# The last gate's weights in two transfers, and ScalarE's group loop as a hardware loop

## The chip, the cores and the metric

The kernel runs on one core of a Trainium2 chip. The metric is the device time of one execution in microseconds. The time before is the median of three runs. The profile is of one more execution, whose own time is given beside its span.

Names used below: PE is TensorE, PEld its weight loads, DVE is VectorE, ACT is ScalarE, POOL is GpSimd, SP is SyncE, which here issues nearly all DMAs. Sixteen DMA engines carry the transfers. Code that an engine has not yet loaded arrives over the same DMA engines, in the profile's queues of kind "instruction".

## What is computed

One decode step of a transformer block for four sequences (B = 4, D = 512), all in f32. A conditioning vector c gives six modulation vectors through one matrix:

```python
mod = (_silu(c) @ w_mod).reshape(c.shape[0], 6, 1, -1)
sa, ca, ga, sb, cb, gb = (mod[:, 0], mod[:, 1], mod[:, 2], mod[:, 3], mod[:, 4], mod[:, 5])
h = _layernorm(x, axis=-1) * (1 + ca) + sa
x = x + ga * _A_ref(h, A_k_cache, A_v_cache, A_wq, A_wo)
h = _layernorm(x, axis=-1) * (1 + cb) + sb
x = x + gb * _B_ref(h, B_w1, B_w3, B_w2)
```

A is attention of one new token over the last 2048 positions of a cache, with 32 query heads of 128 in 8 groups of 4 that share a key and a value head. B is a gated MLP (silu(h w1) * (h w3)) w2 with 1792 hidden columns. The change touches the last gate, gb: columns 2560 to 3071 of w_mod, a product of silu(c) (4 x 512) with a 512 x 512 block.

## The kernel before

**Data and stages.** About 101 MB are read once: for each of the 8 groups 4 MB of keys and 4 MB of values, then the projections, the modulation matrix and the MLP's weights. They arrive in three SBUF buffers: KV[0] and KV[1] (64 KB a partition each), used by even and odd groups, and WP (32 KB) for query and output projections of a pair of groups. In the last stage KV[0] takes the middle modulation weights (wm_in) and w1 with part of w3 (f1_in), KV[1] the rest of w3 (f2_in), the last gate's weights (gb_in, 1 MB) and w2 (w2_in, 3.5 MB in six pieces).

**Who waits for what.** Every engine's program is written out by hand, with semaphores. SP issues the loads in a fixed order (L89 in the helper `load`); before a load that overwrites a buffer it waits until the last reader is done: for WP until the pair's queries are projected (`q_done`) and the pair before has its output projected (`a_done`), for KV until the group's value products are done (`o_done`). PE runs the groups as a hardware loop over four pairs (bodies "pair" and "query"). It takes its inputs with a wait that counts the semaphore down again (`take`, L269), so that one piece of code serves all rounds. DVE and ACT run the eight groups written out one after another (`weights(g)`) and wait on counts that grow from group to group.

**A group.** PE makes the scores (bS), DVE the row maxima and their negative (NB), ACT the exponentials p_sb with their sums (L230), PE turns them (`turn`, L287), DVE places them (pT), PE forms the products with the values (bO, `o_done`), DVE makes the reciprocal sums (LB), ACT scales (o_sb, L251), PE turns the result (bX, `x_done`), DVE picks the diagonal (oT) and PE projects it into bA (`a_done`). For the next group's queries PE projects (bQ, `q_done`), ACT scales (q_sb, L201), PE turns (bT, `qt_done`) and DVE places them into Z (L206).

**The gates.** c comes in t0_in as 16 columns: k-th block of 128 inputs for the 4 sequences. ACT and DVE make silu of it (L182 to L188) in `sc`. For the last gate PE multiplies `sc` block k with block k of the weights into rows 32k to 32k+3 of bank bM, four products of 512 columns side by side (L446). ACT copies bM (L448); a product with the 0/1 matrix `same` later adds the four partial rows up.

**The end.** The six pieces of w2 are consumed in the order of their landing; the partial results of the first eight chunks (bO) are folded (y_sb, `same`) into bX beside the last six. Then DVE multiplies with the gate and adds the residual (L478, L480), SP stores (L482).

Of the kernel before, what the change touches and what calls it, by code (L numbers as in the profile page):

```python
# [5 lines left out]
AF = mybir.ActivationFunctionType  # L6
ALU = mybir.AluOpType
AX = mybir.AxisListType
ET = mybir.EngineType

B, D, HQ, G, SK, DH, W, FF = 4, 512, 32, 8, 8192, 128, 2048, 1792
P = 128
# [2 lines left out]
EPS = 1e-5  # L15
CHUNKS = [(j, c) for c in range(4) for j in range(4) if c < 2 or j < 3]
HEAD = 8
W2_CUTS = [0, 4, 8, 10, 12, 13, 14]
PAIRS = G // 2

# [20 lines left out]
        return (self.sem, self.n)  # L41


def block_kernel(nc, x_in, t0_in, t1_in, kv_in, w_in, wm_in, f1_in, f2_in, gb_in, w2_in, out):
    T, v, s, gp, S = nc.tensor, nc.vector, nc.scalar, nc.gpsimd, nc.sync

    def sems(names):
        return [nc.alloc_semaphore(n) for n in names.split()]

    def sb(name, cols, rows=P):  # L50
        return nc.alloc_sbuf_tensor(name, (rows, cols), F32).ap()
# [5 lines left out]
    A = Queue(nc, s, "act")  # L57
    V = Queue(nc, v, "dve")
    L = Queue(nc, gp, "pool")
    dx, dt0, dt1, dkv, dk, dva, dvb, dwo, dm, df1, df2a, df2b, dgb = sems("dx dt0 dt1 dkv dk dva dvb dwo dm df1 df2a df2b dgb")  # L60
    dw = sems(" ".join(f"dw{i}" for i in range(len(W2_CUTS) - 1)))
    z_ok, q_ok, p_ok, k_ok, va_ok, vb_ok, pt_ok, o_ok, ot_ok = sems("z_ok q_ok p_ok k_ok va_ok vb_ok pt_ok o_ok ot_ok")
    s_done, q_done, qt_done, pp_done, o_done, x_done, a_done, pe, last = sems("s_done q_done qt_done pp_done o_done x_done a_done pe last")
    (dout,) = sems("dout")

    KV = [sb("KV0", 16384), sb("KV1", 16384)]
    WP = sb("WP", 8192)
    T0 = KV[1][:, : 16 + 4096]
    x_sb = sb("x_sb", 512, B)
    ident, same, eps = sb("ident", P), sb("same", B), sb("eps", 1)  # L70
    sc, e1, e2 = sb("sc", 16), sb("e1", 16), sb("e2", 16)
    hT, h2T = sb("hT", 16), sb("h2T", 16)
    Z = sb("Z", B * 28)
    q_sb, p_sb, o_sb, a_sb, y_sb, g_sb, u_sb, gb_sb = [sb(n, 512) for n in "q_sb p_sb o_sb a_sb y_sb g_sb u_sb gb_sb".split()]
# [13 lines left out]
    def load(dst, src, sem):  # L88
        S.dma_start(dst, src).then_inc(sem, 16)  # L89
# [7 lines left out]
    for p in range(PAIRS):  # L97
        if p == PAIRS - 1:
            break
        S.wait_ge(q_done, 2 * p + 2)  # L100
        if p:
            S.wait_ge(a_done, 2 * p)
        if p < PAIRS - 2:
            load(WP, w_in[p], dwo)
        else:
            load(WP, w_in[p], dwo)
        S.wait_ge(o_done, 2 * p + 1)
        load(KV[0], kv_in[2 * p + 2], dkv)
        S.wait_ge(o_done, 2 * p + 2)
        if p < PAIRS - 2:  # L110
            load(KV[1], kv_in[2 * p + 3], dk)
    S.wait_ge(a_done, G - 2)
# [1 line left out]
    load(KV[1][:, :8192], kv_in[G - 1][:, :8192], dk)  # L114
    load(KV[1][:, 8192:14336], kv_in[G - 1][:, 8192:14336], dva)
    load(KV[1][:, 14336:], kv_in[G - 1][:, 14336:], dvb)
    S.wait_ge(o_done, G - 1)
    load(KV[0][:, :6144], wm_in, dm)
    load(KV[0][:, 6144:14336], f1_in, df1)
    S.wait_ge(o_done, G)  # L120
    load(KV[1][:, :3072], f2_in[:, :3072], df2a)
    load(KV[1][:, 3072:6144], f2_in[:, 3072:], df2b)
    load(KV[1][:, 6144:8192], gb_in, dgb)
    for a, b, sem in zip(W2_CUTS[:-1], W2_CUTS[1:], dw):
        load(KV[1][:, 8192 + a * 512 : 8192 + b * 512], w2_in[:, a * 512 : b * 512], sem)


    l_eps = L.op(gp.memset(eps, EPS))
# [50 lines left out]
    v_same = V.op(v.tensor_reduce(same, ident.rearrange("p (j i) -> p i j", i=32)[:, :B, :], axis=AX.X, op=ALU.add))  # L179

    A.wait((dt0, 16))
    t = A.op(s.activation(e1, T0[:, :16], AF.Exp, scale=-1.0))  # L182
    V.wait(t)
    t = V.op(v.tensor_scalar(e2, e1, 1.0, None, op0=ALU.add))
    V.wait(t)
    t = V.op(v.reciprocal(e2, e2))
    V.wait(t, (dt0, 16))
    t_sc = V.op(v.tensor_mul(sc, T0[:, :16], e2))  # L188

    A.wait((pe, 1))  # L190
    t_sa = A.op(s.copy(sa_sb, bM[32 : 32 + B, :]))
# [3 lines left out]
    t_h = V.op(v.scalar_tensor_tensor(h, xs, st1[:, 7:8], sa_sb, op0=ALU.mult, op1=ALU.add))  # L195
    V.wait((pe, 2))
    t_hT = V.op(v.tensor_copy(hT, bT[:, :16]))  # L197

    def q_evac(g):
        A.wait((q_done, g + 1), v_z)  # L200
        A.op(s.mul(q_sb, bQ, DH**-0.5), q_ok)  # L201

    def q_place(g):
        V.wait((qt_done, g + 1), l_z)
# [15 lines left out]
    def weights(g):  # L220
        V.wait((s_done, g + 1), l_z)
        t = V.op(v.reduce_max(MX[:, 0:1], bS, axis=AX.X))  # L222
        V.wait(t)
        t = V.op(v.transpose(MT, MX))
        V.wait(t)
        t = over_t(NM, MT, ALU.max, negate=True)
        V.wait(t)
        t_nm = V.op(v.transpose(NB, NM))  # L228
        A.wait(t_nm)
        A.op(s.activation(p_sb, bS, AF.Exp, bias=NB[:, 0:1], accum_out=SM[:, 0:1]), p_ok)  # L230
        if g % 2 == 0:
            q_evac(g + 1)
        V.wait((pp_done, g + 1))
        V.op(
            v.tensor_copy(  # L235
                pT.rearrange("p (t b c r) -> p c b t r", t=NT, b=B, c=4),
                bP.rearrange("p (c b i) -> p c b i", c=4, b=B)[:, :, :, :16].rearrange("p c b (t r) -> p c b t r", t=NT),
            ),
            pt_ok,
        )  # L240
        if g % 2 == 0:
            q_place(g + 1)
        t = V.op(v.transpose(ST, SM))
        V.wait(t)
        t = over_t(LS, ST, ALU.add)
        V.wait(t)
        t = V.op(v.reciprocal(LR[:, :16], LS[:, :16]))
        V.wait(t)
        t_lb = V.op(v.transpose(LB, LR))
        A.wait((o_done, g + 1), t_lb)  # L250
        A.op(s.mul(o_sb, bO, LB[:, 0:1]), o_ok)  # L251
        V.wait((x_done, g + 1))
        diag = bass.AP(bX.tensor, bX.offset, [list(bX.ap[0]), [1, R], [32, B], [132, 4]])
        V.op(v.tensor_reduce(oT.rearrange("p (r b) -> p r b", r=R), diag, axis=AX.X, op=ALU.add), ot_ok)  # L254
        if g % 2 and g < G - 1:
            q_evac(g + 1)
            q_place(g + 1)

    q_evac(0)
    q_place(0)  # L260
    for g in range(G):
        weights(g)
# [2 lines left out]
    def mm(o, lhsT, rhs, start=True, stop=True):  # L265
        return T.matmul(o, lhsT, rhs, start=start, stop=stop, skip_group_check=True)  # L266
# [38 lines left out]
        ins.then_inc(a_done, 1)  # L305

    root = nc.cur_bb
    reg = T.alloc_register("pairs")
    T.reg_mov(reg, 0)
    T.wait_ge(L.sem, l_z[1])  # L310
    mm(bA, zero[:, :P], zero)
    T.wait_ge(V.sem, t_sc[1])
    for k in range(4):
        for i in range(2):
            ins = mm(bM[32 * i : 32 * i + B, :], sc[:, k * B : (k + 1) * B], T0[:, 16 + (2 * k + i) * 512 : 16 + (2 * k + i + 1) * 512], k == 0, k == 3)
    ins.then_inc(pe, 1)
    T.wait_ge(V.sem, t_h[1])
    for k in range(4):
# [2 lines left out]
    T.wait_ge(V.sem, t_hT[1])  # L321
    T.wait_ge(dt1, 16)
    nc.br("query", engines=[ET.PE])
    nc.br("post", engines=[ET.Activation, ET.DVE, ET.Pool, ET.SP])

    with nc.body("pair", parent=root, valid_engines=[ET.PE]):
        T.reg_add(reg, reg, 1)
# [32 lines left out]
    with nc.body("leave", parent=root, valid_engines=[ET.PE]):  # L360
        T.wait_ge(V.sem, V.n + 1)
        mm(bM[:B, :], same, a_sb).then_inc(pe, 1)
        nc.br("post", engines=[ET.PE])


    nc.switch_bb("post", parent=root)
# [73 lines left out]
    t_hid = V.op(v.tensor_mul(view(hidT)[:, :, :3], view(sT)[:, :, :3], view(bS)[:, :, :3, :B]))  # L440


    T.wait_ge(dgb, 16)
    for k in range(4):
        ins = mm(bM[32 * k : 32 * k + B, :], sc[:, k * B : (k + 1) * B], KV[1][:, 6144 + 512 * k : 6144 + 512 * (k + 1)])
    ins.then_inc(pe, 1)  # L446
    A.wait((pe, 10))
    t_gb = A.op(s.copy(gb_sb, bM))  # L448
    T.wait_ge(V.sem, t_hid[1])
    hw = view(hidT)  # L450
    w2 = KV[1][:, 8192 : 8192 + 14 * 512].rearrange("p (n m) -> p n m", n=14)
    for i in range(len(W2_CUTS) - 1):
        T.wait_ge(dw[i], 16)
        for n in range(W2_CUTS[i], W2_CUTS[i + 1]):
# [32 lines left out]
def _layout(i):  # L487
    import numpy as np

    def a(t):  # L490
        return np.ascontiguousarray(t)

    k = i["A_k_cache"][:, :, SK - W :, :].reshape(B, G, NT, 512, DH)
    v = i["A_v_cache"][:, :, SK - W :, :].reshape(B, G, NT, 4, P, DH)
    k = k.transpose(1, 4, 2, 0, 3).reshape(G, P, 8192)
    v = v.transpose(1, 4, 2, 0, 3, 5).reshape(G, P, 8192)
    wm = i["w_mod"].reshape(4, P, 6, 512).transpose(1, 0, 2, 3)
    c = i["c"].reshape(B, 4, P).transpose(2, 1, 0).reshape(P, 16)
    wq = i["A_wq"].reshape(4, P, G, 512).transpose(2, 1, 0, 3).reshape(G, P, 2048)
    wo = i["A_wo"].reshape(G, R, P, D).transpose(0, 2, 1, 3).reshape(G, P, 2048)  # L500
    pairs = [[wo[2 * p], wo[2 * p + 1]] + ([wq[2 * p + 2], wq[2 * p + 3]] if p < 3 else [wo[6], wo[7]]) for p in range(4)]
    w1 = i["B_w1"].reshape(4, P, FF).transpose(1, 0, 2)
    w3 = i["B_w3"].reshape(4, P, FF).transpose(1, 0, 2)
    w2 = i["B_w2"].reshape(14, P, D)
    return {
        "x_in": a(i["A_x"].reshape(B, D)),
        "t0_in": np.concatenate([c, wm[:, :, 1::-1].reshape(P, 4096)], 1),
        "t1_in": np.concatenate([wq[0], wq[1]], 1),
        "kv_in": np.concatenate([k, v], 2),
        "w_in": np.stack([np.concatenate(p, 1) for p in pairs]),  # L510
        "wm_in": a(wm[:, :, 2:5]).reshape(P, 6144),
        "f1_in": np.concatenate([w1, w3[:, :, 1536:]], 2).reshape(P, 8192),
        "f2_in": a(w3[:, :, :1536]).reshape(P, 6144),
        "gb_in": a(wm[:, :, 5]).reshape(P, 2048),
        "w2_in": a(np.stack([w2[4 * j + c_] for j, c_ in CHUNKS], 1)).reshape(P, 14 * D),
    }

# [14 lines left out]
```

## Time and profile before

| what | value |
|---|---|
| median of three runs | 243.03 us (243.0 to 243.1) |
| the profiled execution's own time, its span | 243.09 us, 241.7 us |
| granted TensorE clock, mean | 0.843 |
| PE busy | 137.8 us, 57% |
| DVE, ACT busy | 38.6 us (16%), 25.1 us (10%) |
| read from HBM | 101.20 MB, 419 GB/s over the span |
| load queue of SP (q1) | 99.17 MB, 95.7% of sixteen engines |
| ACT's two loads (q10) | 2.11 MB, 2.1% |
| code (q8, q14) | 3 and 2 packets, 0.05 and 0.02 MB |

How to read it: the span runs from the first to the last instruction. A DMA row gives packets, megabytes and the share of the time of all sixteen engines. In a windows row stand the window, its length, each engine's busy time with its count of instructions, the granted clock, the share of the sixteen DMA engines and GB/s. In a timeline row stand start, length, engine, line, operation, tiles and count, and in brackets the idle time before and who ended it.

### The profile page before, as it was taken

What the parts mean: (1) busy time and instruction counts of PE and PEld (TensorE: products, weight loads), DVE (VectorE), ACT (ScalarE), POOL (GpSimd) and SP (SyncE); (2) the same over time, 40 slices, a digit from 0 to 9 for tenths busy, and PEclk for the clock granted to TensorE, in tenths of its full rate; (3) what the DMA queues carried; (4) which work ended last, traced back from release to release, by engine and by line L of the source; (5) the groups of instructions that cost most, each with busy time, mean ns of one, the idle gap of its engine ahead of it and who ended that gap; (6) DMA issues with size and microseconds to landing.
All of it is one profiled execution on the core that took longest, in us unless ns stands there. A gap on an engine that the chain in (4) does not pass through costs nothing. (4 is left out here: it accounts for less than half of the span.)

```text
span 241.7 us, 2238 instructions
## 1 busy us (share of the span) xinstructions
PE 137.8 (57%) x940; PEld 38.0 (16%) x940; DVE 38.6 (16%) x126; ACT 25.1 (10%) x54; POOL 1.7 (1%) x14
## 2 busy tenths in 40 slices
PE   3004677726771478267713782877137869656964
PEld 0000122201220013112200130121001312111211
DVE  3003203202200022022000220130002222133112
ACT  2002002100010011010100110011002100133110
POOL 2000000000000000000000000000000000000000
PEclk9999959968798579887985898679758997995999
DMA  7998989899989898999898989998989999999993
GB/s 266 440 511 358 510 361 499 369 423 439 504 369 499 369 499 370 423 428 504 369 499 369 499 369 423 434 510 369 499 347 445 442 396 445 449 431 394 413 415 116
DMA packets 4045, 101.34 MB, mean 419 GB/s; under 512 B 452, under 2 KB 580, under 8 KB 1096
## 3 DMA queue, kind: packets, MB, share of 16 engines
q1 hardware_dynamic: 3888, 99.17, 95.7%
q10 hardware_dynamic: 152, 2.11, 2.1%
q8 instruction: 3, 0.05, 0.1%
q14 instruction: 2, 0.02, 0.0%
HBM read 101.20 MB, written 0.07 MB: 419 GB/s over the span
## 5 line engine op out<-in xcount | busy, mean ns | idle before, releaser
L266 PE MATMUL bS<-KV,Z 128*16 128x512 f32 x256 | 42.7, 828 | 39.2 <-PEq L269 39.2
L266 PE MATMUL bO<-KV,pT 128*16 128x512 f32 x256 | 32.5, 652 | 0.5
L266 PEld LDWEIGHTS bS<-KV,Z 128*16 128x16 f32 x256 | 9.3, 123 | 67.1 <-issue 67.1
L222 DVE TENSOR_REDUCE MX<-bS 128x1 f32<-128x512 f32 x8 | 5.5, 692 | 80.4 <-PE bS L266 80.4
L266 PE MATMUL bM<-KV,sc 128*4 128x512 f32 x24 | 6.9, 801 | 16.6 <-DVE sc L188 16.6
L230 ACT ACTIVATE p_sb<-bS,NB 128x512 f32<-128x512 f32 x8 | 5.5, 687 | 101.2 <-DVE NB L228 101.2
L287 PE MATMUL bP<-ident,p_sb 128*128 128x128 f32 x32 | 5.6, 303 | 16.6 <-PEq L269 16.6
L266 PE MATMUL bA<-WP,oT 128*4 128x512 f32 x64 | 11.1, 773 | 4.3 <-PEq L269 4.3
L266 PEld LDWEIGHTS bO<-KV,pT 128*16 128x16 f32 x256 | 8.2, 107 | 23.9 <-issue 23.9
L251 ACT ACTIVATE o_sb<-bO,LB 128x512 f32<-128x512 f32 x8 | 5.5, 687 | 48.8 <-PE bO L266 48.8
L266 PE MATMUL bQ<-WP,hT 128*4 128x512 f32 x64 | 9.2, 647 | 0.6 <-DVE hT L197 0.6
L287 PE MATMUL bX<-ident,o_sb 128*128 128x128 f32 x32 | 5.0, 280 | 7.2 <-PEq L269 7.2
L254 DVE TENSOR_REDUCE oT<-bX 128x16 f32<-128x64 f32 x8 | 1.8, 224 | 43.6 <-PE bX L287 43.6
L287 PEld LDWEIGHTS bP<-ident,p_sb 128*128 128x128 f32 x32 | 3.6, 148 | 24.0 <-issue 24.0
L287 PE MATMUL bT<-ident,q_sb 128*128 128x128 f32 x32 | 5.5, 298 | 3.2 <-PEq L269 3.2
L201 ACT ACTIVATE q_sb<-bQ 128x512 f32<-128x512 f32 x8 | 4.7, 593 | 13.3 <-PE bQ L266 13.3
L287 PEld LDWEIGHTS bX<-ident,o_sb 128*128 128x128 f32 x32 | 3.4, 141 | 14.3 <-issue 14.3
L235 DVE COPY pT<-bP 128x256 f32<-128x256 f32 x8 | 3.4, 424 | 13.5 <-PE bP L287 13.5
L266 PE MATMUL bQ<-KV,h2T 128*4 128x512 f32 x32 | 5.3, 816 | 0.3 <-DVE h2T L398 0.3
L287 PEld LDWEIGHTS bT<-ident,q_sb 128*128 128x128 f32 x32 | 3.6, 150 | 8.0 <-issue 7.7
L266 PEld LDWEIGHTS bM<-KV,sc 128*4 128x4 f32 x24 | 1.0, 104 | 22.4 <-DVE sc L188 18.2
L266 PE MATMUL bX<-KV,sc 128*4 128x512 f32 x24 | 4.2, 592 | 0.0
(100 smaller groups left out, 65.2 us busy)
## 6 DMA issues: line engine op xcount, KB each, us to landing
WP<-w_in SPq DMA_DIRECT2D x3, 4096.0 KB, 22.0
KV<-kv_in SPq DMA_DIRECT2D x1, 4096.0 KB, 24.3
KV<-f_in SPq DMA_DIRECT2D x1, 4096.0 KB, 28.0
KV<-kv_in SPq DMA_DIRECT2D x1, 3072.0 KB, 31.1
KV<-wm_in SPq DMA_DIRECT2D x1, 3072.0 KB, 18.4
KV<-f_in SPq DMA_DIRECT2D x2, 1536.0 KB, 19.2
KV<-t_in SPq DMA_DIRECT2D x1, 2056.0 KB, 12.2
WP<-t_in ACTq DMA_DIRECT2D x1, 2048.0 KB, 12.4
```

The lines of the kernel that those rows point to most:

```text
L201: A.op(s.mul(q_sb, bQ, DH**-0.5), q_ok)
L222: t = V.op(v.reduce_max(MX[:, 0:1], bS, axis=AX.X))
L230: A.op(s.activation(p_sb, bS, AF.Exp, bias=NB[:, 0:1], accum_out=SM[:, 0:1]), p_ok)
L235: v.tensor_copy(pT.rearrange("p (t b c r) -> p c b t r", t=NT, b=B, c=4), bP.rearrange("p (c b i) -> p c b i", c=4, b=B)[:, :, :, :16].rea ...
L251: A.op(s.mul(o_sb, bO, LB[:, 0:1]), o_ok)
L254: V.op(v.tensor_reduce(oT.rearrange("p (r b) -> p r b", r=R), diag, axis=AX.X, op=ALU.add), ot_ok)
L266: return T.matmul(o, lhsT, rhs, start=start, stop=stop, skip_group_check=True)
L287: ins = T.transpose(dst[:, c * P : (c + 1) * P], src[:, c * P : (c + 1) * P], ident)
```

## The change

**The last gate's weights.** Columns 0 to 319 (GA) stay as they were, four blocks of 128 rows side by side. The other 192 (GB) of the 512 input rows are cut otherwise: the first 128 rows as one block of 128 partitions (they follow in gb_in), the other 384 as four blocks of 96 partitions. These four lie in gc_in, 96 partitions of 768 columns, stored in HBM as 12 slices of 9 rows of which 8 are read, so that the source has an outermost size of 12. Both transfers count on `dgb`. For the blocks of 96, `sc` needs c cut the same way: t0_in carries 16 more columns. PE forms the gate with nine products instead of four. w2 lies 192 columns further on in KV[1].

**ACT's groups.** ACT's part of `weights` becomes a hardware loop over pairs ("act_pair"), with waits that count down. Since ACT now counts `q_done` and `o_done` down, SP waits for `qt_done` and `x_done` in their place, and DVE signals the maxima and the reciprocal sums on semaphores of their own (`nm_ok`, `lb_ok`).

```diff
+GA = 320
+GB = 512 - GA
+W2_AT = 8192 + GB
...
-        S.wait_ge(q_done, 2 * p + 2)
+        S.wait_ge(qt_done, 2 * p + 2)
...
-        S.wait_ge(o_done, 2 * p + 1)
+        S.wait_ge(x_done, 2 * p + 1)
         load(KV[0], kv_in[2 * p + 2], dkv)
-        S.wait_ge(o_done, 2 * p + 2)
+        S.wait_ge(x_done, 2 * p + 2)
...
-    S.wait_ge(o_done, G - 1)
+    S.wait_ge(x_done, G - 1)
...
-    S.wait_ge(o_done, G)
+    S.wait_ge(x_done, G)
...
-    load(KV[1][:, 6144:8192], gb_in, dgb)
+    load(KV[1][:, 6144 : 6144 + 4 * GA + GB], gb_in, dgb)
+    load(KV[1][:96, 6144 + 4 * GA + GB : 8192 + GB], gc_in[:, :8], dgb)
...
-    t = A.op(s.activation(e1, T0[:, :16], AF.Exp, scale=-1.0))
+    t = A.op(s.activation(e1, T0[:, :32], AF.Exp, scale=-1.0))
...
-        t_nm = V.op(v.transpose(NB, NM))
-        A.wait(t_nm)
-        A.op(s.activation(p_sb, bS, AF.Exp, bias=NB[:, 0:1], accum_out=SM[:, 0:1]), p_ok)
-        if g % 2 == 0:
-            q_evac(g + 1)
+        V.op(v.transpose(NB, NM), nm_ok)
...
-        t_lb = V.op(v.transpose(LB, LR))
-        A.wait((o_done, g + 1), t_lb)
-        A.op(s.mul(o_sb, bO, LB[:, 0:1]), o_ok)
+        V.op(v.transpose(LB, LR), lb_ok)
...
+    def atake(*sems_):
+        for s_ in sems_:
+            s.wait_ge(s_, 1).then_inc(s_, -1)
+
+    with nc.body("act_pair", parent=root, valid_engines=[ET.Activation]):
+        s.reg_add(areg, areg, 1)
+        for odd in range(2):
+            if not odd:
+                atake(q_done)
+                A.op(s.mul(q_sb, bQ, DH**-0.5), q_ok)
+            atake(nm_ok)
+            A.op(s.activation(p_sb, bS, AF.Exp, bias=NB[:, 0:1], accum_out=SM[:, 0:1]), p_ok)
+            if not odd:
+                atake(q_done)
+                A.op(s.mul(q_sb, bQ, DH**-0.5), q_ok)
+            atake(lb_ok, o_done)
+            A.op(s.mul(o_sb, bO, LB[:, 0:1]), o_ok)
+        s.br_lt(areg, PAIRS, on_true="act_pair", on_false="post")
...
-    T.wait_ge(dgb, 16)
-    for k in range(4):
-        ins = mm(bM[32 * k : 32 * k + B, :], sc[:, k * B : (k + 1) * B], KV[1][:, 6144 + 512 * k : 6144 + 512 * (k + 1)])
+    T.wait_ge(dgb, 32)
+    for k in range(4):
+        mm(bM[32 * k : 32 * k + B, :GA], sc[:, k * B : (k + 1) * B], KV[1][:, 6144 + GA * k : 6144 + GA * (k + 1)])
+    mm(bM[:B, GA:], sc[:, :B], KV[1][:, 6144 + 4 * GA : 6144 + 4 * GA + GB], True, False)
+    for k in range(4):
+        at = 6144 + 4 * GA + GB * (k + 1)
+        ins = mm(bM[32 * k : 32 * k + B, GA:], sc[:96, 16 + k * B : 16 + (k + 1) * B], KV[1][:96, at : at + GB], k > 0, True)
...
+    gc = np.zeros((12, 9, 4 * GB), wg.dtype)
+    gc[:, :8] = i["w_mod"][P:, 5 * 512 + GA : 6 * 512].reshape(4, 96, GB).transpose(1, 0, 2).reshape(12, 8, 4 * GB)
```

More of the change, by code (lines that the diff above doesn't have):

```diff
@@ L41, in op, with block_kernel @@
         return (self.sem, self.n)
-def block_kernel(nc, x_in, t0_in, t1_in, kv_in, w_in, wm_in, f1_in, f2_in, gb_in, w2_in, out):
+def block_kernel(nc, x_in, t0_in, t1_in, kv_in, w_in, wm_in, f1_in, f2_in, gb_in, gc_in, w2_in, out):
     T, v, s, gp, S = nc.tensor, nc.vector, nc.scalar, nc.gpsimd, nc.sync
@@ L63, in block_kernel @@
     s_done, q_done, qt_done, pp_done, o_done, x_done, a_done, pe, last = sems("s_done q_done qt_done pp_done o_done x_done a_done pe last")
-    (dout,) = sems("dout")
+    (nm_ok, lb_ok, dout) = sems("nm_ok lb_ok dout")
     KV = [sb("KV0", 16384), sb("KV1", 16384)]
     WP = sb("WP", 8192)
-    T0 = KV[1][:, : 16 + 4096]
+    T0 = KV[1][:, : 32 + 4096]
     x_sb = sb("x_sb", 512, B)
     ident, same, eps = sb("ident", P), sb("same", B), sb("eps", 1)
-    sc, e1, e2 = sb("sc", 16), sb("e1", 16), sb("e2", 16)
+    sc, e1, e2 = sb("sc", 32), sb("e1", 32), sb("e2", 32)
     hT, h2T = sb("hT", 16), sb("h2T", 16)
@@ L116, in block_kernel @@
     load(KV[1][:, 14336:], kv_in[G - 1][:, 14336:], dvb)
-    S.wait_ge(o_done, G - 1)
+    S.wait_ge(x_done, G - 1)
     load(KV[0][:, :6144], wm_in, dm)
     load(KV[0][:, 6144:14336], f1_in, df1)
-    S.wait_ge(o_done, G)
+    S.wait_ge(x_done, G)
     load(KV[1][:, :3072], f2_in[:, :3072], df2a)
     load(KV[1][:, 3072:6144], f2_in[:, 3072:], df2b)
-    load(KV[1][:, 6144:8192], gb_in, dgb)
+    load(KV[1][:, 6144 : 6144 + 4 * GA + GB], gb_in, dgb)
+    load(KV[1][:96, 6144 + 4 * GA + GB : 8192 + GB], gc_in[:, :8], dgb)
     for a, b, sem in zip(W2_CUTS[:-1], W2_CUTS[1:], dw):
-        load(KV[1][:, 8192 + a * 512 : 8192 + b * 512], w2_in[:, a * 512 : b * 512], sem)
+        load(KV[1][:, W2_AT + a * 512 : W2_AT + b * 512], w2_in[:, a * 512 : b * 512], sem)
     l_eps = L.op(gp.memset(eps, EPS))
@@ L187, in block_kernel @@
     V.wait(t, (dt0, 16))
-    t_sc = V.op(v.tensor_mul(sc, T0[:, :16], e2))
+    t_sc = V.op(v.tensor_mul(sc, T0[:, :32], e2))
     A.wait((pe, 1))
@@ L197, in block_kernel @@
     t_hT = V.op(v.tensor_copy(hT, bT[:, :16]))
-    def q_evac(g):
-        A.wait((q_done, g + 1), v_z)
-        A.op(s.mul(q_sb, bQ, DH**-0.5), q_ok)
     def q_place(g):
@@ L255, in weights @@
         if g % 2 and g < G - 1:
-            q_evac(g + 1)
             q_place(g + 1)
-    q_evac(0)
+    A.wait(v_z, l_z)
     q_place(0)
@@ L307, in block_kernel @@
     root = nc.cur_bb
-    reg = T.alloc_register("pairs")
+    reg, areg = T.alloc_register("pairs"), s.alloc_register("act_pairs")
     T.reg_mov(reg, 0)
+    s.reg_mov(areg, 0)
     T.wait_ge(L.sem, l_z[1])
@@ L314, in block_kernel @@
         for i in range(2):
-            ins = mm(bM[32 * i : 32 * i + B, :], sc[:, k * B : (k + 1) * B], T0[:, 16 + (2 * k + i) * 512 : 16 + (2 * k + i + 1) * 512], k == 0, k == 3)
+            ins = mm(bM[32 * i : 32 * i + B, :], sc[:, k * B : (k + 1) * B], T0[:, 32 + (2 * k + i) * 512 : 32 + (2 * k + i + 1) * 512], k == 0, k == 3)
     ins.then_inc(pe, 1)
@@ L323, in block_kernel @@
     nc.br("query", engines=[ET.PE])
-    nc.br("post", engines=[ET.Activation, ET.DVE, ET.Pool, ET.SP])
+    nc.br("act_pair", engines=[ET.Activation])
+    nc.br("post", engines=[ET.DVE, ET.Pool, ET.SP])
     with nc.body("pair", parent=root, valid_engines=[ET.PE]):
@@ L450, in block_kernel @@
     hw = view(hidT)
-    w2 = KV[1][:, 8192 : 8192 + 14 * 512].rearrange("p (n m) -> p n m", n=14)
+    w2 = KV[1][:, W2_AT : W2_AT + 14 * 512].rearrange("p (n m) -> p n m", n=14)
     for i in range(len(W2_CUTS) - 1):
@@ L498, in _layout @@
     c = i["c"].reshape(B, 4, P).transpose(2, 1, 0).reshape(P, 16)
+    c96 = np.zeros((P, 16), c.dtype)
+    c96[:96] = i["c"].reshape(B, 512)[:, P:].reshape(B, 4, 96).transpose(2, 1, 0).reshape(96, 16)
+    wg = wm[:, :, 5]
+    gc = np.zeros((12, 9, 4 * GB), wg.dtype)
+    gc[:, :8] = i["w_mod"][P:, 5 * 512 + GA : 6 * 512].reshape(4, 96, GB).transpose(1, 0, 2).reshape(12, 8, 4 * GB)
     wq = i["A_wq"].reshape(4, P, G, 512).transpose(2, 1, 0, 3).reshape(G, P, 2048)
@@ L506, in _layout @@
         "x_in": a(i["A_x"].reshape(B, D)),
-        "t0_in": np.concatenate([c, wm[:, :, 1::-1].reshape(P, 4096)], 1),
+        "t0_in": np.concatenate([c, c96, wm[:, :, 1::-1].reshape(P, 4096)], 1),
         "t1_in": np.concatenate([wq[0], wq[1]], 1),
@@ L513, in _layout @@
         "f2_in": a(w3[:, :, :1536]).reshape(P, 6144),
-        "gb_in": a(wm[:, :, 5]).reshape(P, 2048),
+        "gb_in": np.concatenate([a(wg[:, :, :GA]).reshape(P, 4 * GA), wg[:, 0, GA:]], 1),
+        "gc_in": gc,
         "w2_in": a(np.stack([w2[4 * j + c_] for j, c_ in CHUNKS], 1)).reshape(P, 14 * D),
```

## The prediction

> **What bounds the kernel now.** I read the page's DMA part first, then the chain that ended last, then the busy share of the sixteen DMA engines in the last microseconds. From the page:
>
> ```profile
> span 241.7 us, 2238 instructions
> ...
> DMA packets 4045, 101.34 MB, mean 419 GB/s; under 512 B 452, under 2 KB 580, under 8 KB 1096
> ...
> q1 hardware_dynamic: 3888, 99.17, 95.7%
> q10 hardware_dynamic: 152, 2.11, 2.1%
> q8 instruction: 3, 0.05, 0.1%
> q14 instruction: 2, 0.02, 0.0%
> ```
>
> The engines are busy 98% of the span; bytes set the time. The two instruction queues carry five packets of code. The end of the chain of waits:
>
> ```profile
> 210.14 28.79 DMA KV<-w_in
> ...
> 239.77 0.29 DVE y L480
> ```
>
> The last w2 piece lands 28.79 us after its issue, at 238.93, and 1.1 us of work, the store and its landing follow it. So the question is when the last piece of w2 lands. It lands when the slowest of sixteen engines is through. The windows view of that stretch (length; busy time of PE, PEld, DVE, ACT, POOL; clock; share of the sixteen engines; GB/s):
>
> ```profile
> 224.00:234.00 10.00, 8.68 (x76) 2.12 (x64) 2.02 (x6) 1.40 (x3) 0.00 (x0) 1.00 1.00 415
> 236.20:236.60 0.40, 0.16 (x9) 0.15 (x12) 0.33 (x1) 0.00 (x0) 0.00 (x0) 1.00 1.10 410
> 237.25:237.50 0.25, 0.17 (x8) 0.00 (x0) 0.00 (x0) 0.00 (x0) 0.00 (x0) 1.00 0.25 98
> 237.56:237.82 0.26, 0.11 (x4) 0.11 (x8) 0.00 (x0) 0.00 (x0) 0.00 (x0) 1.00 0.18 71
> 237.90:238.26 0.36, 0.36 (x16) 0.14 (x8) 0.00 (x0) 0.00 (x0) 0.00 (x0) 1.00 0.12 46
> 238.32:238.48 0.16, 0.13 (x8) 0.11 (x8) 0.00 (x0) 0.00 (x0) 0.00 (x0) 1.00 0.07 26
> 238.60:238.90 0.30, 0.16 (x8) 0.00 (x0) 0.00 (x0) 0.00 (x0) 0.00 (x0) 1.00 0.00 0
> ```
>
> A sixteenth is 0.0625. Full until 236.6; from 237.25 on, four engines still work, then three, two, one, none. Reading the steps between the windows, the four end at about 237.53, 237.85, 238.29 and 238.50, and twelve between 236.6 and 237.25. One engine moves 415/16 = 26 GB/s (26 in the row of one). **So the kernel's end is set by one late engine, 1.25 us after the last of the twelve.**
>
> Why late? The DMA view of five narrow windows (33.80 to 33.99, then 0.2 us each from 91.9, 206.5, 213.3 and 236.9) holds the five code packets; share times 16 times the window is the duration:
>
> ```profile
> q8 instruction: 1, 0.02, 33.9%
> ...
> q14 instruction: 1, 0.01, 10.4%
> ...
> q14 instruction: 1, 0.01, 9.7%
> ...
> q8 instruction: 1, 0.02, 34.3%
> ...
> q8 instruction: 1, 0.02, 34.2%
> ```
>
> 1.03, 0.33, 0.31, 1.10 and 1.09 us. Four of them fall before the tail, two long, two short; the tail has four late engines, two very late, two less. Each packet sits on one engine, whose data waits behind it, and as the queue never empties nothing is made up. I take q8 as PE's code, PE having most of the instructions, and the two short ones by what was awake:
>
> ```profile
> 91.94 0.23 DVE L206 TENSOR_REDUCE Z<-bT 128x16 f32<-128x64 f32 x1
> ...
> 206.46 0.69 ACT L251 ACTIVATE o_sb<-bO,LB 128x512 f32<-128x512 f32 x1 [6.89 <-PE bO L266]
> ```
>
> At 92.0 VectorE was working, at 206.6 ScalarE and SyncE had just been released; I take DVE and ACT. The fifth, at 237.0, moved none of the four steps: it fell on an engine that was through.
>
> **The change, part by part.** (1) *Gate weights.* Bytes are the same: 128 x 1472 x 4 + 96 x 768 x 4 = 1,048,576. What changes is who carries them. Before, each engine took 8 rows x 8192 B. After, each takes 8 x 5888 B, and the new transfer's twelve slices give twelve engines 8 x 3072 B more: +6,144 B on twelve, -18,432 B on four, at 26 GB/s **+0.24 and -0.71 us**. That a transfer of n slices uses n engines is seen in x_in, of four rows:
>
> ```profile
> q10 hardware_dynamic: 4, 0.01, 7.0%
> ```
>
> That is the window 14.5 to 14.8: four packets of 2 KB, and q10's 152 are 128 + 16 of t1_in and 4 + 4 of x_in. [...]
>
> Which of the late ones are among the relieved four is therefore bounded: each ends 0.71 earlier or 0.24 later. By place alone a given engine is relieved 4 times in 16. I take the two PE ones as relieved and the DVE one as loaded: q8's three refills hit three engines, which looks like a group kept for PE's code, apart from q14's. That is a choice, not a reading. Then: PE's 238.50 - 0.71 = 237.79 and 237.58; DVE's 237.85 + 0.24 = **238.09**; the twelve 237.49 at most. The end moves from 238.50 to 238.09, **-0.41**.
>
> (2) *ACT's loop.* Its code becomes one pair instead of four, so the refill at 206.6 should go, and with it the lag of the engine at 237.53. That one is not last: worth 0 here; if the refill stays, 237.53 + 0.24 = 237.77, also not last. The added semaphore instructions run in groups of some 20 us, 8.39 MB at 419 GB/s, of which ACT is busy for a few passes of 0.69; they cost nothing while the loads take that long.
>
> (3) *SP's waits* move from L266's ends to those of the transposes. By rows:
>
> ```profile
> 1.16 26.33 SPq L89 DMA_DIRECT2D KV<-kv_in  x2
> 39.50 0.33 SPq L89 DMA_DIRECT2D WP<-w_in  x1
> 46.00 23.31 SPq L89 DMA_DIRECT2D KV<-kv_in  x2
> ...
> 41.58 0.63 PE L287 MATMUL bT<-ident,q_sb 128*128 128x128 f32 x4
> ...
> 46.84 0.63 PE L287 MATMUL bX<-ident,o_sb 128*128 128x128 f32 x4 [0.89 <-PEq L269]
> ...
> KV<-f_in SPq DMA_DIRECT2D x2, 1536.0 KB, 19.2
> ...
> KV<-kv_in SPq DMA_DIRECT2D x7, 32.2
> ```
>
> The load released at 46.00 goes out at 47.47, 1.5 us later; the WP load, released at 39.5, at 42.2, 2.7 later. Moving 8 MB takes 20 us, and landing takes 32.2: 12 us of queue stand ahead. For f2_in (1.5 MB, 3.8 us) 15 us. So 0; beyond 10 us the queue would run dry, each microsecond then costing one. The gate and w2 issues behind it on SP slip as far, with one issue of 0.43 us more:
>
> ```profile
> 207.77 12.21 SPq L89 DMA_DIRECT2D KV<-w_in  x6
> ```
>
> Five issues at 0.47 (0.43 and the step between) leave 9.8 us for the sixth: it stood until 220. With one more ahead two may stand; their data is wanted after 236.
>
> (4) *Gate matmuls*, four of 512 columns become nine (four of 320, five of 192):
>
> ```profile
> 231.47 1.04 PE L266 MATMUL bM<-KV,sc 128*4 128x512 f32 x8
> ...
> 235.16 1.04 PE L266 MATMUL bO<-KV,hidT 128*4 128x512 f32 x8 [1.14 <-DMA KV<-w_in]
> ...
> 236.44 0.62 PE L266 MATMUL bX<-KV,hidT 128*4 128x128 f32 x16 [0.24 <-DMA KV<-w_in]
> ...
> 237.02 0.40 PE L266 MATMUL bX<-y_sb,same 128*4 128x128 f32 x8
> ```
>
> Eight passes become 18: by columns +0.1, by passes +1.3 us. PE waits 1.14 us for the second piece of w2, so it hides nearly all at either end; what is left over, at most 0.5, ends before the later pieces land.
>
> (5) *t0_in* grows by 64 B a row, 8 KB: 8192/415 GB/s = **+0.02**. Exp, add, reciprocal and product on 32 columns instead of 16: from nothing to +0.5 each (a 512-column pass takes ACT 0.69), at most 2 us ahead of the second KV load. That one went out at 27.2, while the 12.6 MB asked for before it last until 1.2 + 12.6/0.419 = 31 us: 4 us of cover.
>
> **Sum.** -0.41 + 0.02 = -0.39 us. The profiled execution took 243.09 for its span of 241.7, the median is 243.03: 242.70 by the first, **242.64** by the median.
>
> **The rivals.** *(a) PE's latest engine is loaded* (likeliest by place alone: 12 of 16). 238.50 + 0.24: +0.24 + 0.02, **243.29**. If only the 238.29 one is loaded it ends at 238.53, 243.08.
>
> *(b) PE's last refill now lands in the way.* It came near 237.0, as the y_sb passes began; the nine gate matmuls put 20 PE instructions ahead of it (two loads and two passes for each of five more), so it falls into the 16-pass group at 236.44, right behind the third piece's landing, when every engine has two pieces of w2 left. On a loaded engine: 236.6 to 237.25, + 0.24, + 1.1 (the packet) to 1.65 (238.29 - 236.6, what such a refill has cost at most) = 237.9 to 239.1, the middle 238.5: nothing gained, **243.05**, with up to +0.6. For it: the order of the code. Against: on a relieved engine it comes when that one is through, as now.
>
> *(c) All late ones are relieved.* Then 237.79 is last: -0.71 + 0.02, **242.34**.
>
> *(d) ACT's loop fetches its code again*, the slower side. If the branch back draws an 8 KB refill in each of four rounds on one engine, that engine loses 4 x p, p between 0.31 (packet) and 0.9 (237.53 - 236.6); it decides from 237.1 + 0.24 + 4p > 238.5, p > 0.29. At p = 0.6: 239.7, +1.2, **244.2**. Against it: PE's loop turns back three times between 60 and 206 us, and q8 has three packets in all, none in that time. [...]
>
> **How the numbers follow.** Chances: forecast 0.36, (a) 0.27, (b) and other ends within 0.15 of now 0.19, (c) 0.12, (d) 0.06. A measurement of this kernel tells 0.2%, 0.49 us, from no change. Faster by that: (c) and the forecast's lower edge, 0.19; slower: (d) and (b)'s upper end, 0.09; within, 0.72. The range 242.25 to 243.55 leaves out (d) and part of (b) and (c); the forecast's own is 242.5 to 242.85.
>
> **What would show it.** The share steps after the twelve: two late engines fewer or closer, the last step near 238.1; q14 with one packet, not two; SP's KV issues 1.5 us later and landing 1.5 us sooner after them; q8's third packet ahead of the y_sb passes. Wrong if the last step stands at 238.7 (a), if a q8 packet is followed by a new late engine (b), or if q14 has more than two packets (d).

## The result, and the profile after

The kernel after took **244.57 us** (median of 5, 243.68 to 245.19), the kernel before beside it on the same chip 243.03 (243.00 to 243.17): a ratio of 1.0057, 95% interval 1.0033 to 1.0081. It is 1.5 us slower; forecast were 242.64, and a range that ended at 243.55.

The profiled execution is the fastest of the five, 243.68 us for a span of 242.3 (before: 243.09 for 241.7), so it shows only +0.59 of the +1.54. From its page, the span and the queues (packets, MB, share of sixteen engines):

```profile
span 242.3 us, 2292 instructions
...
q1 hardware_dynamic: 3996, 99.17, 95.9%
...
q8 instruction: 3, 0.05, 0.1%
q14 instruction: 1, 0.01, 0.0%
```

The bytes are the same, and one of the two packets of q14 is gone. q1 has 3996 packets in place of 3888, 108 more: 96 of 3072 bytes, one a row, and 12 of 4 bytes (packets under 512 bytes: 464 in place of 452). Of these small ones a load of 128 rows has 16 in both traces, and x_in with its four rows has 4. Taken as one an engine, the new load runs on twelve engines, as was put. The end of its chain of waits (start, length):

```profile
219.19 20.39 DMA KV<-w_in
```

The last piece of w2 lands at 219.19 + 20.39 = 239.58, where it was 238.93: the end is still set there, 0.65 us later. So one looks for where the loads lost time. The windows view of the kernel before over the four microseconds in which the gate's weights and the head of w2 are on the way (length; busy time of five engines; clock; DMA share; GB/s):

```profile
227.00:231.00 4.00, 2.94 (x23) 0.74 (x17) 1.82 (x5) 0.22 (x1) 0.00 (x0) 1.00 1.01 422
```

and of the kernel after, the same four microseconds and then one by one, with the six before them:

```profile
227.00:231.00 4.00, 2.85 (x19) 0.72 (x16) 1.71 (x5) 0.22 (x1) 0.00 (x0) 1.00 1.02 308
220.00:226.00 6.00, 5.73 (x41) 1.31 (x43) 0.17 (x1) 0.26 (x1) 0.00 (x0) 0.70 0.99 420
226.00:227.00 1.00, 1.00 (x12) 0.11 (x6) 0.00 (x0) 0.33 (x1) 0.00 (x0) 1.00 1.04 432
227.00:228.00 1.00, 0.49 (x4) 0.12 (x2) 0.00 (x0) 0.00 (x0) 0.00 (x0) 1.00 1.07 332
228.00:229.00 1.00, 1.00 (x10) 0.50 (x13) 0.17 (x1) 0.22 (x1) 0.00 (x0) 1.00 1.13 264
229.00:230.00 1.00, 1.00 (x12) 0.10 (x4) 0.90 (x4) 0.00 (x0) 0.00 (x0) 1.00 0.90 268
230.00:231.00 1.00, 0.36 (x3) 0.00 (x0) 0.65 (x2) 0.00 (x0) 0.00 (x0) 1.00 0.99 369
231.00:232.00 1.00, 0.84 (x12) 0.56 (x13) 0.31 (x2) 0.00 (x0) 0.00 (x0) 1.00 1.04 434
```

The share column stays at one, the GB/s column falls from 432 to 264. The engines are not idle; each packet takes longer: of those that start between 228 and 229 one of 8192 bytes takes 0.59 us (the median; 0.31 in the kernel before), one of 5888 bytes 0.38 (0.23 from 226 to 227), one of 3072 bytes 0.21 (the shortest of that size in the trace 0.12). What is lost is (422 - 308) x 4 / 422 = **1.08 us**, all of it there. That is what has to be explained.

The tail, in the same view of the kernel after (a sixteenth is 0.0625):

```profile
237.60:237.80 0.20, 0.20 (x14) 0.11 (x8) 0.02 (x1) 0.00 (x0) 0.00 (x0) 1.00 0.88 328
238.40:238.50 0.10, 0.10 (x6) 0.10 (x10) 0.00 (x0) 0.00 (x0) 0.00 (x0) 1.00 0.27 102
238.60:238.90 0.30, 0.30 (x16) 0.11 (x4) 0.00 (x0) 0.00 (x0) 0.00 (x0) 1.00 0.14 55
238.98:239.12 0.14, 0.12 (x7) 0.10 (x8) 0.00 (x0) 0.00 (x0) 0.00 (x0) 1.00 0.04 15
239.20:239.40 0.20, 0.20 (x8) 0.00 (x0) 0.00 (x0) 0.00 (x0) 0.00 (x0) 1.00 0.00 0
```

A row counts a packet whole in the window in which it starts, so over a tenth of a microsecond it can show one engine too many. The packets themselves, which the trace keeps with start and length, follow one another without a gap on an engine (at the end one of 2048 bytes every 0.08 us), and so give the ends: three late engines are left where there were four, at 238.59, 238.98 and 239.13; the others are through by 238.35. The forecast was 238.09, and 238.09 + 1.08 = 239.17; the two that it took as relieved, 237.58 and 237.79, come to 238.66 and 238.87 in the same way.

The rest of the after page answers the side steps. From its timeline, SP's issues and the gate and w2 passes:

```profile
42.19 0.33 SPq L92 DMA_DIRECT2D WP<-w_in  x1
49.24 21.60 SPq L92 DMA_DIRECT2D KV<-kv_in  x2
...
145.34 0.33 SPq L92 DMA_DIRECT2D KV<-kv_in  x1
...
208.89 0.43 SPq L92 DMA_DIRECT2D KV<-gb_in  x1
209.36 0.94 SPq L92 DMA_DIRECT2D KV<-gc_in  x1
...
231.64 1.35 PE L259 MATMUL bM<-KV,sc 128*4 128x320 f32 x18
...
235.82 1.04 PE L259 MATMUL bO<-KV,hidT 128*4 128x512 f32 x8 [1.14 <-DMA KV<-w_in]
...
237.11 0.62 PE L259 MATMUL bX<-KV,hidT 128*4 128x128 f32 x16 [0.25 <-DMA KV<-w_in]
```

from the page, the two f2_in loads (19.2 us before):

```profile
KV<-f_in SPq DMA_DIRECT2D x2, 1536.0 KB, 17.7
```

and from the DMA view of the window 237.20 to 237.45, PE's third code packet:

```profile
q8 instruction: 1, 0.02, 27.6%
```

They are read point by point further down.

### The profile page after: what moved, and what is told of

Its sections match the earlier page's. It is cut to its first block, busy times and chain, and to the rows that moved or that the text cites. A ratio compares the mean times of both kernels' runs of the same rounds, so it can differ in the third digit from the quotient of the medians.

```text
span 242.3 us, 2292 instructions
## 1 busy us (share of the span) xinstructions
PE 138.7 (57%) x950; PEld 38.7 (16%) x950; DVE 38.8 (16%) x126; ACT 25.1 (10%) x54; POOL 1.7 (1%) x14
## 3 DMA queue, kind: packets, MB, share of 16 engines
q1 hardware_dynamic: 3996, 99.17, 95.9%
## 5 line engine op out<-in xcount | busy, mean ns | idle before, releaser
L259 PE MATMUL bS<-KV,Z 128*16 128x512 f32 x256 | 42.1, 817 | 36.9 <-PEq L262 36.7
L259 PE MATMUL bO<-KV,pT 128*16 128x512 f32 x256 | 33.5, 669 | 0.5
L259 PE MATMUL bM<-KV,sc 128*4 128x512 f32 (+3 forms) x34 | 7.2, 618 | 16.6 <-DVE sc L192 16.6
L259 PEld LDWEIGHTS bM<-KV,sc 128*4 128x4 f32 (+1 forms) x34 | 1.4, 99 | 22.7 <-DVE sc L192 18.2
L206 DVE TENSOR_REDUCE Z<-bT 128x16 f32<-128x64 f32 x8 | 1.8, 225 | 15.4 <-PE bT L280 15.1
## 6 DMA issues: line engine op xcount, KB each, us to landing
KV<-f_in SPq DMA_DIRECT2D x2, 1536.0 KB, 17.7
```

The lines of the kernel that those rows point to most:

```text
L206: v.tensor_reduce(Z.rearrange("p (b i) -> p b i", b=B)[:, :, 12 : 12 + R], bT.rearrange("p (r k i) -> p i r k", r=R, k=4)[:, :B], axis=AX. ...
```

## The experiments

What a kernel "lost" is, below, worked out as above: (422 - the row's GB/s) x length / 422.

### The parts alone, and two other shapes of the second load

*loop_only* is the kernel after with the gate's edits taken back: ACT's loop and SP's later waits alone. *gate_only* is the kernel before with the gate's edits alone.

> ACT's loop and SP's later waits alone; the last gate's weights stay one transfer of 128 rows as before. If the slowdown comes from the gate's transfer: no change, 242.9 to 243.15 us, one q14 packet instead of two, the four late engines three. If it comes from the loop or from SP's later issues: 244 us or more, with its spread of 1.5 us.

> The gate's two transfers alone; ACT written out and SP's waits as before. If the gate's transfer is the cause: 243.6 to 245.2 us like the changed kernel, with 195 to 345 GB/s in 227.5 to 230.5 us. If loop and gate only hurt together: 242.6 us.

*gate_96* and *gate_128* are the kernel after with another second load:

```diff
-    load(KV[1][:96, 6144 + 4 * GA + GB : 8192 + GB], gc_in[:, :8], dgb)    # 12 slices of 8 rows
+    load(KV[1][:96, 6144 + 4 * GA + GB : 8192 + GB], gc_in, dgb)           # gate_96: 96 rows, unsliced
+    load(KV[1][:, 6144 + 4 * GA + GB : 6144 + 4 * GA + GB + 576], gc_in, dgb)   # gate_128: 128 rows x 576
```

> The changed kernel with the 96 rows stored as one plain block, so that the source has an outermost size of 96 and the transfer goes to sixteen engines, six rows each. Theory port (engines that write to the same part of SBUF at one time share its speed): 96 rows still fall askew on the engines, so a smaller stall, 243.3 to 244.3. Theory source (the padded 12 by 9 rows in HBM are slow to read) and theory twelve (any transfer on twelve engines is slow): no stall, 243.0 to 243.1, as nobody is relieved.

> The changed kernel with the same 288 KB spread over 128 rows of 576 columns; the gate's products still read 96 rows of 768 columns, so the last gate is computed from wrong places, the work and the bytes stay. Theory port: 128 rows fall on the engines as all other loads do, no stall, 242.95 to 243.15. Theory small transfer (a second transfer of short rows, or its issue, costs): 243.6 or more.

Measured: loop_only 243.06, ratio 0.9999 (0.9989 to 1.0008); gate_only 244.87, 1.0079 (1.0062 to 1.0096); gate_96 244.47, 1.0057 (1.0040 to 1.0074); gate_128 243.19, 1.0005 (0.9995 to 1.0014). The windows view of the four, in this order:

```profile
227.00:231.00 4.00, 4.00 (x28) 0.91 (x22) 1.13 (x4) 0.78 (x2) 0.00 (x0) 1.00 1.01 420
```

```profile
227.00:231.00 4.00, 2.81 (x19) 0.72 (x16) 1.36 (x5) 0.22 (x1) 0.00 (x0) 1.00 1.02 300
```

```profile
227.00:231.00 4.00, 3.46 (x25) 0.77 (x19) 1.58 (x5) 0.22 (x1) 0.00 (x0) 1.00 1.03 302
```

```profile
227.00:231.00 4.00, 3.01 (x23) 0.74 (x17) 1.82 (x5) 0.22 (x1) 0.00 (x0) 1.00 1.03 417
```

The loss comes with the gate's load alone. It is not the loop, not SP's later issues, not the use of twelve engines (gate_96 has no slices and loses 1.14 us as well, where a smaller loss was expected), not the padding between the slices, and not that there is a second, smaller load: gate_128 has the same 288 KB as a second load, issued at the same place, and loses 0.05. What separates it from the slow ones is 128 rows against 96. Its gate products still read 96 rows of 768 columns, so they do not form the gate, as in twelve_108 and twelve_120 below; work and bytes stay.

gate_128 showed something by the way. Its profiled execution took 243.43, 0.34 more than that of before. The DMA view of 237.1 to 237.4 has PE's third code packet; then two rows of the tail, and the last piece of w2 in the chain of waits:

```profile
q8 instruction: 1, 0.02, 22.8%
```

```profile
238.50:238.55 0.05, 0.05 (x8) 0.03 (x7) 0.00 (x0) 0.00 (x0) 0.00 (x0) 1.00 0.10 41
238.65:238.85 0.20, 0.17 (x8) 0.00 (x0) 0.00 (x0) 0.00 (x0) 0.00 (x0) 1.00 0.00 0
```

```profile
220.03 19.32 DMA KV<-w_in
```

The data are through at 238.59, hardly later than the 238.52 of before, and no late engine has a gap in its packets that the code packet could have made. But the last piece lands at 239.35, 0.76 after the data, where it was 0.41 in the kernel before and 0.45 in the kernel after. By the trace's packets one engine had its data through at 237.21, just as the code packet began, and wrote its completion only at 238.29, as it ended; the other fifteen completions of that piece have landed by 239.00, so the one at 239.35 is put down to this engine. That is the mechanism of rival (b), and about its size, with a completion held up in place of data.

### Nine and ten rows to a slice, two halves, and a mended split

The next theory was of collisions inside the second load alone, by how its own rows fall to the engines. Which rows collide in it was the author's assumption; no trace shows it. *twelve_108* and *twelve_120* keep twelve slices and the bytes, with nine and ten rows of fewer columns to a slice (`gc_in[:, :9]` of 684 columns onto 108 rows; `gc_in[:, :10]` of 616 onto 120). *gate_108* is made by the theory, with nine rows to a slice and no stall expected; it cuts the gate's weights so that 108 rows hold what they should: 384 columns as 128 rows, 128 columns as 80 rows and four times 108. *halves_64* is the kernel before with its gate load cut in two by rows:

```diff
-    load(KV[1][:, 6144:8192], gb_in, dgb)
+    load(KV[1][:64, 6144:8192], gb_in[:64], dgb)
+    load(KV[1][64:, 6144:8192], gb_in[64:], dgb)
...
-    T.wait_ge(dgb, 16)
+    T.wait_ge(dgb, 32)
```

> The changed kernel with the twelve slices of 9 rows of 684 columns instead of 8 rows of 768: 108 rows, the same bytes within 0.2%, still twelve engines. The gate's products read 96 rows of 768 columns as before, so the last gate is computed from wrong places; work and bytes stay. [...] Theory twelve (a transfer on twelve engines is slow as such): 243.7 to 245.2 us.

> The same with 10 rows of 616 columns: 120 rows. [...] Theory twelve: 243.7 to 245.2.

> The kernel before with one edit: the 1 MB of the last gate goes in two transfers of 64 rows, sixteen engines and rows of 8192 B each, instead of one of 128 rows. [...] Theories of twelve engines, short rows or a padded source: 243.0 to 243.1.

> [...] The relieved engines carry 12,288 B less, the others 6,144 more. Theory port: no stall; the latest of PE's engines from 238.50 to 238.03, DVE's from 237.85 to 238.09, so 242.6 to 242.75 us. Theory twelve: 243.5 or more.

Measured: twelve_108 244.80, 1.0077 (1.0060 to 1.0094); twelve_120 244.16, 1.0054 (1.0037 to 1.0070); gate_108 244.41, 1.0049 (1.0032 to 1.0067); halves_64 247.93, 1.0190 (1.0168 to 1.0211). The windows view of twelve_108, of gate_108, and of halves_64:

```profile
227.00:231.00 4.00, 4.00 (x33) 1.10 (x28) 0.75 (x2) 0.81 (x2) 0.00 (x0) 1.00 1.03 318
```

```profile
227.00:231.00 4.00, 3.69 (x25) 0.82 (x19) 1.39 (x5) 0.44 (x2) 0.00 (x0) 1.00 1.03 344
```

```profile
226.00:230.00 4.00, 2.61 (x24) 0.38 (x12) 0.00 (x0) 0.59 (x1) 0.00 (x0) 1.00 0.97 190
230.00:234.00 4.00, 3.03 (x20) 1.09 (x20) 1.93 (x6) 0.22 (x1) 0.00 (x0) 1.00 1.02 238
```

The theory fell: spreading the rows within the second load does not take the loss away, so gate_108, made by it, didn't either. halves_64 was the most telling. No slices, no short rows, no bytes more, all sixteen engines in use (16 packets more, the completions of the second load), and 2.20 + 1.74 = 3.94 us lost in eight. The author's estimate by the theory, which rests on that assumption, was 1.5 to 2.5 us; it is 4.9 slower. Two theories were left. *Row count*: a load of fewer than 128 rows is slow. *Rows*, a guess of the author's: in a load of 128 rows each engine writes eight rows of its own; a load that is dealt out otherwise makes engines write into rows that are another's in the loads beside it, and that is what collides.

### The same rows dealt out otherwise, and the same slices on other rows

Three runs tell these two apart. *sliced_128* is the kernel before with its 1 MB to the same 128 rows in one load, but read from 16 slices of 8 rows:

```diff
-    load(KV[1][:, 6144:8192], gb_in, dgb)
+    load(KV[1][:, 6144:8192], gb_in[:, :8], dgb)      # gb_in is (16, 9, 2048), the ninth row padding
```

*rows_0_32* and *rows_64_96* are the kernel before with one added load, and the wait on `dgb` raised for it; they differ in nothing but its rows:

```diff
+    load(KV[0][0:32, 14336:16384], gx_in[:, :4], dgb)       # rows_0_32; gx_in is (8, 5, 2048)
+    load(KV[0][64:96, 14336:16384], gx_in[:, :4], dgb)      # rows_64_96
```

> The kernel before, with one edit: the gate's 1 MB lies in memory as 16 slices of 8 rows with a ninth row of padding behind each, and is loaded as 16 x 8 rows into the same 128 rows. Nothing is left out and no byte more is moved. Theory of the rows (each DMA engine has its own eight of the 128 rows, and a load whose rows are dealt out in another way makes engines write into each other's part): if the slices are dealt out as they lie, eight neighbouring rows to an engine, the whole 1 MB collides, and the time is 2 to 5 us longer (245.0 to 248.0; halves_64, the same bytes, took 4.9). Theory of the row count (a load of 128 rows is fine however it lies, one of fewer rows is slow): no change, 242.8 to 243.3. If the chip deals out 128 rows in its own way whatever the source looks like, the theory of the rows expects no change either, and then this run doesn't tell them apart.

> The kernel before, with an added load of 256 KB (zeros, used for nothing) between the gate's weights and w2: 8 slices of 4 rows x 8192 B, onto rows 0 to 31 of free space. Eight engines get four more packets of 8192 B, some 1.25 us at 309 ns for one in the trace of before; the other eight get none. [...] Theory of the row count: 32 rows, eight engines, so slow like the loads of 64 to 120 rows: 244.3 to 246.

> As rows_0_32, the same 256 KB in the same eight slices, but onto rows 64 to 95. [...] Theory of the row count: the same time as rows_0_32 within 0.3 us.

Measured in one series: sliced_128 247.30, 1.0167 (1.0147 to 1.0187); rows_0_32 243.55, 1.0027 (1.0016 to 1.0039); rows_64_96 245.86, 1.0127 (1.0104 to 1.0149). The windows view of sliced_128:

```profile
226.00:230.00 4.00, 2.67 (x20) 0.39 (x12) 0.00 (x0) 0.59 (x1) 0.00 (x0) 0.98 0.99 202
230.00:234.00 4.00, 2.51 (x17) 0.76 (x17) 1.82 (x5) 0.22 (x1) 0.00 (x0) 1.00 1.00 246
234.00:238.00 4.00, 1.81 (x16) 0.58 (x20) 0.20 (x1) 0.59 (x1) 0.00 (x0) 0.80 0.98 399
```

of rows_0_32:

```profile
228.00:232.00 4.00, 3.20 (x28) 0.92 (x26) 2.02 (x6) 0.22 (x1) 0.00 (x0) 1.00 1.02 424
```

and of rows_64_96:

```profile
227.00:228.00 1.00, 1.00 (x12) 0.19 (x6) 0.00 (x0) 0.53 (x1) 0.00 (x0) 1.00 1.09 442
228.00:232.00 4.00, 3.20 (x24) 0.93 (x19) 1.82 (x5) 0.22 (x1) 0.00 (x0) 1.00 1.01 233
232.00:236.00 4.00, 2.30 (x24) 0.57 (x26) 0.20 (x1) 0.59 (x1) 0.00 (x0) 1.00 0.99 409
```

The row count is out. The kernel becomes 4.3 us slower with a load of the same 128 rows and bytes, on sixteen engines as before (3888 packets in both), that is read in 16 slices: that it is dealt out otherwise is inferred, as no row numbers the engines. A load of 32 rows runs at the full 424 GB/s on rows 0 to 31 and at 233, with all that goes beside it, on rows 64 to 95, with the same eight slices read from the same place: 2.3 us between the medians. Reading is the same in both, and sliced and padded in both, so it is the writing side.

While the load onto rows 64 to 95 is on the way, a packet of 8192 bytes takes 0.62 us (the median from 228 to 230) in place of 0.31, and 233 of 424 GB/s is 0.55 of the rate. The author's forecasts by the theory of the rows, 243.0 to 243.7 for rows_0_32 and 1 to 2.5 us more for rows_64_96, hold. But that the first load collides with nothing and the second does was put in as an assumption: no trace shows which engine writes which row.

### A split with two loads of 32 rows

The last run is the kernel after with a smaller part taken out of the gate's weights: 448 columns as 128 rows x 1792, the last 64 columns as two loads of 8 slices x 4 rows x 2048 B onto rows 0 to 31 and 32 to 63. Eight groups of matmuls over 64 rows each stand in place of one over 128 and four over 96. The slices of four rows are taken over from rows_0_32; that rows 32 to 63 do as well as 0 to 31 is assumed. The edit:

```diff
-GA = 320
+GA = 448
...
-    load(KV[1][:96, 6144 + 4 * GA + GB : 8192 + GB], gc_in[:, :8], dgb)
+    load(KV[1][:32, GC_AT:W2_AT], gc_in[0, :, :4], dgb)
+    load(KV[1][32:64, GC_AT:W2_AT], gc_in[1, :, :4], dgb)
...
+    for k in range(4):
+        for h in range(2):
+            at = GC_AT + GB * (4 * h + k)
+            ins = mm(bM[32 * k : 32 * k + B, GA:], sc[:64, 16 * h + k * B : 16 * h + (k + 1) * B], KV[1][:64, at : at + GB], h == 0, h == 1)
```

> [...] Nothing is left out. Eight engines carry 8 KB less than in the kernel before, eight 8 KB more, 0.31 us each way at 309 ns for 8192 B. Theory of the rows: no stall; the latest engines (two at 238.29 and 238.50, with the last landing at 238.93) are among those relieved, the late one among those loaded ends at 237.85 + 0.31 = 238.16: the end is 0.2 to 0.35 us sooner, 242.65 to 242.9, unless the third refill of code makes another engine late, 243.2. Theory of the row count: two loads of 32 rows, 128 KB in all, are half a stall like the one of the change: 243.6 or more.

Measured: 242.95 us (median of 11, 242.59 to 243.68), ratio 1.0001 (0.9992 to 1.0010). The windows view, with the tail:

```profile
227.00:231.00 4.00, 4.00 (x28) 0.91 (x22) 1.13 (x4) 0.81 (x2) 0.00 (x0) 1.00 1.02 417
237.30:237.50 0.20, 0.07 (x4) 0.07 (x8) 0.00 (x0) 0.00 (x0) 0.00 (x0) 1.00 0.24 92
237.90:238.10 0.20, 0.20 (x12) 0.05 (x8) 0.00 (x0) 0.00 (x0) 0.00 (x0) 1.00 0.18 72
238.15:238.35 0.20, 0.20 (x8) 0.01 (x1) 0.00 (x0) 0.00 (x0) 0.00 (x0) 1.00 0.00 0
```

The loss is gone: 417 GB/s, with three loads in place of one and two of them onto 32 rows. The interval lies wholly under that of the kernel after. In its profiled execution (242.71, 0.38 under that of before) the last engines stop at 238.19, near the 238.16 foreseen, against 238.52 before. That does not hold over the eleven runs: their median is 0.11 under that of before, inside the interval, and above the 242.65 to 242.9 foreseen. Only the profiled run has a trace, so what makes an engine late in the slower ones stays open. With these rows, then, taking bytes out of the 128-row load into smaller ones costs nothing that shows (417 GB/s, ratio 1.0001), and one execution shows the end come sooner; that the kernel gains by it is not shown.

## Why the prediction was wrong, point by point

**(1), the gate's weights: the step that failed.** It priced the new transfer as "+6,144 B on twelve, -18,432 B on four, at 26 GB/s". The bytes and the twelve engines stand (108 packets more), though no run shows which four are relieved; the rate does not. While the 96-row load is in flight every engine, the four relieved ones too, runs at about 264/422 of its rate (from 228 to 229 every packet of data takes longer: 0.48 to 0.61 us for 8192 bytes where it was 0.31 to 0.32, 0.34 to 0.43 for 5888 where it was 0.23, 0.17 to 0.25 for 3072 where the shortest was 0.12), which costs 1.08 us in the profiled execution and about 2 us at the median, if (244.57 - 243.03) + 0.39 is taken as its price there. The sum then closes: -0.41 foreseen + 1.08 = +0.67, against +0.65 measured at the last landing.

The choice made in that step, PE's late engines relieved and the DVE one loaded, fits: with PE's latest loaded the last step would be 238.50 + 0.24 + 1.08 = 239.82, and it is at 239.13. The three late ends, 238.59, 238.98 and 239.13, are within 0.11 of 238.66, 238.87 and 239.17. It is a fit and not a reading of engines, and the choice had been a guess.

What was missing is a bound. The trace of before has no load of fewer than 128 rows in the full stream: x_in, four rows at 14.5 us, was quoted for how many engines it takes, and says nothing of what it does to others. The 26 GB/s came from rows of 128-row loads, and the term went into the sum with its sign uncertain and its rate not.

**(2), ACT's loop: right.** q14 has one packet in place of two, and the loop with SP's waits is worth 0.9999 (0.9989 to 1.0008). loop_only has three late engines by its packets (237.63, 238.37 and 238.61) where the kernel before has four, as expected: with ACT's code packet at 206.6 one late engine went too.

**(3), SP's waits: right in what they cost.** WP's load goes out at 42.19, 2.7 us after 39.50 as foreseen. The KV load released at 46.00 before goes out at 49.24, 3.2 us later where 1.5 was put: the 32 value products ahead of it took 5.32 us in place of 3.63, with a granted clock of 0.68 in place of 1.00 from 42.3 to 47.6. A later one goes out at 145.34, 1.5 after the 143.80 of before. f2_in lands 17.7 us after its issue in place of 19.2, 1.5 sooner. The queue never ran dry: 420 GB/s from 220 to 226. SP needs 0.94 us for the sliced load where 0.43 was put; the slack took that too.

**(4), the gate's matmuls: right.** 18 passes take 1.35 us in place of 1.04, +0.31 inside the +0.1 to +1.3 given, and PE still waits 1.14 us for the second piece of w2.

**(5), t0_in:** its 0.02 us is too little for any of these runs to show; gate_128, which has it, is at 1.0005.

**The rivals.** (a) gave 243.29 and (b) up to 243.65, both for the order in which late engines end; the place of the loss was neither. (b)'s mechanism showed in one trace: in the kernel after the third code packet came at the foreseen place, behind the third piece of w2 (237.11), and began as one engine ended (237.29) and held up nothing; in gate_128, where it took 1.09 us, it held up a completion by the account above, 0.35 us past the next latest one. (d) was wrong: one q14 packet in four rounds of the loop. No rival had the loads themselves slow down, so no chance stood for what happened, and "a transfer that disturbs others" has to be among the rivals wherever a load of a new shape joins a full stream.

## What to carry to other kernels

In a kernel whose DMA engines are full, ask of each load not only how many bytes each engine moves but which rows it writes, and in what slices. With loads of 128 rows in flight, the loads that slowed nothing here were full 128 rows unsliced (417 GB/s in gate_128) and eight slices of four onto rows 0 to 31 (424 in rows_0_32), or onto rows 0 to 31 and 32 to 63 (417 in own_rows). With every other one the sixteen engines together fell, while it lasted, to between 190 and 344 GB/s of about 422. The mark in a profile is a DMA share that stays near 1.00 (0.97 to 1.03 here) while GB/s falls. An edit that shifts bytes between engines is best tried at first by its bytes alone, in a load that is used for nothing, before matmuls are cut to fit it.

## What the runs showed of the hardware

- **The slow stretch is longer than the odd load.** sliced_128 reads 1.05 MB in slices; the slow stretch from 226 to 234 moves (202 + 246) x 4 us = 1.79 MB. The ordinary packets of w2 that run beside the odd ones are slowed too: in the kernel after, 0.59 us for 8192 bytes (the median from 228 to 229) in place of 0.31.
- **Half the rate, and a loss beyond what the added load accounts for.** In rows_64_96 a packet of 8192 bytes takes 0.62 us (the median) from 228 to 230, and 0.31 before. An engine's 32 KB of the added load, 1.25 us at 0.31 a packet, would be over in 2.5 us at 0.62 and cost 1.25. The loss is (424 - 233) x 4 / 424 = 1.8 us, and halves_64 is 4.9 slower where the author's estimate had been up to 2.5. In the kernel after, engines that carry none of the odd packets slow down as well: at 229.0 all sixteen packets under way are slow, eleven of 8192 bytes at 0.54 to 0.61 us, two of 5888 at 0.40 and 0.43, three of 3072 at 0.23 to 0.25. Why it is more stays open: the trace has no row for it.
- **Such kernels spread.** The kernel after ran from 243.68 to 245.19 and sliced_128 from 246.75 to 247.98, the kernel before within 0.5 us in the same series. A single profile of such a kernel can show little more than a third of its median loss, as here.
- **A sliced load takes longer to issue.** SP took 0.94 us for twelve slices of eight rows, 0.83 for eight of four (rows_64_96), 0.64 for sixteen of eight (sliced_128), and 0.43 for a plain load, of 96 rows (gate_96) as of 128.
